# Running the last two units of each layer inside the hardware loop, and keeping the third buffer place for weights, in a two-layer decode kernel

## The chip, the cores and the metric

One core of one Trainium2 chip. The time is the device time of one execution in microseconds (us), the median of several executions. All executions told of here were of the fast state, with a mean granted TensorE clock of 0.669 to 0.675. PE is the matrix engine, ACT and DVE are the scalar and the vector engine, and SP is the engine that issues the loads.

## The reference, cut to what matters

Two layers. Each is attention of one new token over a long cache, followed by a small MLP. There are 2 batches of 32 heads, 64 units of (batch, head) in all, and each unit reads a K and a V of 16384 x 128 bf16, 4 MB each.

```python
def _A_ref(x, k_cache, v_cache, wq, wo):            # B=2, Sq=1, D=576, H=32, Sk=16384, Dh=128
    q = (x @ wq).reshape(B, Sq, H, Dh).transpose(0, 2, 1, 3)
    scores = jnp.einsum("bhqd,bhkd->bhqk", q, k_cache) * (Dh ** -0.5)
    o = jnp.einsum("bhqk,bhkd->bhqd", _softmax(scores), v_cache)
    return o.transpose(0, 2, 1, 3).reshape(B, Sq, H * Dh) @ wo
x = x + _A_ref(_layernorm(x), A_k_cache, A_v_cache, A_wq, A_wo)
x = x + _B_ref(_layernorm(x), B_w1, B_w2, B_w3, B_w4)     # with S = 1, w2 meets only zeros
# ... and both lines once more: the second layer reads the same caches and weights
```

The caches are read twice, except for two units that the second layer finds still in the buffer. That makes 1098 MB of loads with almost no arithmetic per byte.

## The kernel before: what the change and the argument touch

The buffer has three places, each with room for one K and one V. A load is issued by SP, in one fixed order, as soon as the last reader of the bytes under it is done (`Arena.pump`). All loads go to one queue of the DMA.

```python
def place(self, l, i):                    # l: layer, i: position of the unit in the layer
    if i == self.U - 1:
        return 2 - 2 * l                  # the last unit takes the third place
    if l == 0:
        return i % 2
    return (2, 0, 1)[i % 3] if i < self.ROT else (2, 1)[i % 2]      # ROT = 7
# ... (cut) in plan(), the order of the loads:
    for i in range(U):
        kv("K", l, i, ...)
        if l == 1 and i < self.EARLY:     # EARLY = 9: V of a unit right behind its K ...
            kv("V", l, i)
        elif i >= 1 and (l, i - 1) != (1, self.EARLY - 1):
            kv("V", l, i - 1)             # ... later K one unit ahead of V
        if i % 8 == 0 and 8 <= i <= 8 * self.n_wo:
            want_wo(l, i // 8 - 1, wp * self.place_n)    # a piece of wo for 4 heads
    # ... (cut)
    kv("V", l, U - 1, (2, 1, 1))
    want_w34(l, 1, 1 if l == 0 else 2)    # w3, then w4 in four pieces; pieces 2 to 4 lie over w3
```

K of a unit is cut into 16 groups of 8 blocks of 128 rows. PE and ACT do 9 or 10 of these groups (transpose the 8 blocks, evict, multiply with q), while DVE does the rest of the 16 as dot products. Then come the maximum, the exponentials, and 128 small "weighing" matmuls with V. Two units are one turn of a hardware loop on PE, ACT and DVE; units 0 to 1 of layer 1, units 0 to 7 of layer 2, and units 62 and 63 of both are straight-line code.

```python
def attention(self, l):
    first = (2, self.EARLY - 1)[l]
    self.s.loops.append((l * U + first, (U - 2 - first) // 2, 2, ...))
    for i in range(U):
        # ... (cut) turns; weigh(l, i - 1) inside unit i, but not inside the last unit:
        now = i >= 1 and not early and i < U - 1
        # ... (cut)
        if i % 8 == 1 and 9 <= i <= 8 * self.n_wo + 1:
            self.project_piece(l, i // 8 - 1)      # multiplies with a piece of wo
        if i == U - 2:
            self.project_mid(l)
    self.unit_max(l, U - 1)
    self.exps(l, U - 1)
    # ... (cut)
    self.weigh(l, U - 2, 0)
    self.weigh(l, U - 2, 1)
    self.weigh(l, U - 1, 0)
    self.weigh(l, U - 1, 1)
    # ... (cut) then the last head of wo, then the MLP
```

## Time and profile before

| | before |
|---|---|
| time, median of the 3 runs known at the prediction | 2566.87 us |
| span of the profiled run | 2565.0 us |
| data moved by the data queue | 1097.76 MB, 99.8% of the 16 engines' span |
| instruction blocks fetched | 48 of 16 KB |
| rate in undisturbed slices | 431 to 433 GB/s |

The page, kernel before. The first line gives busy us, share and count for each engine; GB/s is the mean over all DMA engines in 40 slices of 64 us; the queue lines give packets, MB and share of 16 engines' time.

```profile
PE 1652.4 (64%) x36879; PEld 1539.2 (60%) x36879; DVE 1750.1 (68%) x2587; ACT 1229.8 (48%) x1941; POOL 0.8 (0%) x10
...
GB/s 414 429 429 431 432 433 430 431 432 432 430 432 431 432 432 432 432 431 431 424 413 429 423 418 432 431 433 431 432 431 432 431 431 433 431 431 431 433 431 375
...
q1 hardware_dynamic: 46712, 1097.76, 99.8%
q8 instruction: 48, 0.79, 0.1%
```

No compute engine is over 68% busy, and the data queue is full. The weak slices are the first, the ones around the change of layers (20 to 24) and the last. Next the timeline of PE at the end of layer 1 (start, length, line, instruction, count; in brackets the idle time ahead of it and what ended it):

```profile
1271.94 5.61 PE L799 MATMUL ops<-p,buf 128*128 128x1 bf16 x205
1279.56 1.52 PE L799 MATMUL ops<-p,buf 128*128 128x1 bf16 x51 [2.02 <-issue]
1281.34 0.29 PE L632 MATMUL misc<-otn,wolast 128*128 128x2 bf16 x5 [0.26 <-DVE otn L821]
1282.09 0.61 PE L562 MATMUL misc<-xa,small 128*128 128x16 f32 x2 [0.46 <-DVE xa L557]
```

After the last exponentials, PE weighs V of units 62 and 63 in one run of 256 matmuls, with a gap of 2.02 us in which nothing in the trace was being waited for. Only then can the MLP begin (L562, at 1282.09). What the DMA did meanwhile, in the table of stretches (each engine's busy us and count, then PE clock, DMA share, GB/s):

```profile
1286.00:1290.00 4.00, 2.12 (x65) 2.00 (x64) 0.99 (x7) 0.50 (x2) 0.00 (x0) 0.50 0.92 374
1290.00:1294.00 4.00, 2.83 (x107) 2.74 (x103) 0.51 (x3) 0.49 (x2) 0.00 (x0) 0.50 0.77 243
```

The rate falls to 243 GB/s: the second piece of w4 has to wait until the MLP has read w3. The queue's own timeline shows when the last K, two V and w3 were issued:

```profile
1212.21 0.43 SPq L403 DMA_DIRECT2D buf<-in_A_k_cache_dram  x1
1229.93 0.33 SPq L403 DMA_DIRECT2D buf<-in_A_v_cache_dram  x1
1253.84 1.28 SPq L400 DMA_DIRECT2D buf<-in_A_v_cache_dram  x3
1255.16 2.99 SPq L417 DMA_DIRECT2D buf<-in_B_w_dram  x5
```

K of unit 63 goes out at 1212.21, well ahead; V of unit 63 (three parts) waits until 1253.84. Finally layer 2: the end of PE's multiplication with the first piece of wo after unit 9, and two of the four stretches of 20 us from 1440 to 1520 (the other two show 415 and 413):

```profile
1483.12 0.69 PE L632 MATMUL misc<-orows,buf 128*128 128x2 bf16 x20 [0.39 <-DVE orows L883]
1484.77 1.89 PE L726 MATMUL tps<-ident,buf 128*128 128x128 bf16 x16 [0.95 <-DVE xa L841]
```

```profile
1440.00:1460.00 20.00, 12.41 (x275) 11.82 (x275) 13.49 (x19) 9.65 (x15) 0.00 (x0) 0.67 0.98 413
1460.00:1480.00 20.00, 12.30 (x275) 11.72 (x275) 13.35 (x19) 9.65 (x15) 0.00 (x0) 0.67 0.99 417
```

PE's product with wo (L632) waits for DVE, not for the load. The rate is about 414 GB/s for 80 us, where 432 is normal. I read this as 3 us lost.

### The profile page before, as it was taken

The page shows a single profiled execution, that of the slowest core. Times are in us where ns is not written, and L with a number is a line of the kernel's source. Part 1 is how long each engine was busy: PE and PEld are TensorE (multiplying, and loading weights), DVE is VectorE, ACT ScalarE, POOL GpSimd, SP SyncE. Part 2 cuts the span into 40 slices and gives each one's busy share as a digit, 9 for nine tenths or more (in the row PEclk, how much of TensorE's full clock was granted, in tenths as well). Part 3 has the DMA queues.
Part 4 walks back from the last instruction along what each step waited for, and adds up shares of the span by engine and source line. Part 5 has one row for each costly group of instructions (what it writes and reads, how often), then busy time and mean ns, then how long its engine had stood idle before and what let it go on. Part 6 is the DMA issues. An engine that isn't in the chain of part 4 may idle for free.

```text
span 2565.0 us, 84163 instructions
## 1 busy us (share of the span) xinstructions
PE 1652.4 (64%) x36879; PEld 1539.2 (60%) x36879; DVE 1750.1 (68%) x2587; ACT 1229.8 (48%) x1941; POOL 0.8 (0%) x10
## 2 busy tenths in 40 slices
PE   5656666666566666656668676666656665666566
PEld 5555665566565656655668665555655655565565
DVE  5666767677666767766658677766766766677664
ACT  4444544454455445544436555444544544454452
POOL 0000000000000000000000000000000000000000
PEclk8666666676667666766656667666666766676665
DMA  9999999999999999999999999999999999999998
GB/s 414 429 429 431 432 433 430 431 432 432 430 432 431 432 432 432 432 431 431 424 413 429 423 418 432 431 433 431 432 431 432 431 431 433 431 431 431 433 431 375
DMA packets 46770, 1098.63 MB, mean 428 GB/s; under 512 B 4916, under 2 KB 6008, under 8 KB 11512
## 3 DMA queue, kind: packets, MB, share of 16 engines
q1 hardware_dynamic: 46712, 1097.76, 99.8%
q8 instruction: 48, 0.79, 0.1%
q14 instruction: 10, 0.08, 0.0%
HBM read 1097.74 MB, written 0.00 MB: 428 GB/s over the span
## 4 chain that ended last, share of the span: by engine, by line
DMA 57%; issue 16%; DVE 16%; PE 8%; SPq 1%; ACT 1%; DVEq 0%
DMA buf<-in_A_k_cache_dram 56%; DVE prod L755 12%; PE tps L726 5%; DVE sd L758 3%; PE misc L774 2%; SPq L434 1%; PE ops L799 1%; DMA buf<-in_B_w_dram 1%; DMA buf<-in_A_wq_dram 1%; SPq L417 0%; ACT ktsb L730 0%; PE misc L632 0%; DVE small L776 0%; PE sps L596 0%; PE sps L743 0%
## 5 line engine op out<-in xcount | busy, mean ns | idle before, releaser
L730 ACT ACTIVATE ktsb<-tps 128x1024 bf16<-128x1024 bf16 x1156 | 1123.3, 1031 | 879.9 <-PE tps L726 875.3
L726 PE MATMUL tps<-ident,buf 128*128 128x128 bf16 x9248 | 908.1, 262 | 619.8 <-DMA buf<-in_A_k_cache_dram 606.9
L726 PEld LDWEIGHTS tps<-ident,buf 128*128 128x128 bf16 x9248 | 732.1, 120 | 648.4 <-DMA buf<-in_A_k_cache_dram 626.4
L758 DVE TENSOR_REDUCE sd<-prod 128x8 f32<-128x1024 bf16 x892 | 1088.0, 1220 | 30.9
L755 DVE TENSOR_TENSOR prod<-buf,qb 128x1024 bf16<-128x1024 bf16 x892 | 607.5, 681 | 11.1 <-DMA buf<-in_A_k_cache_dram 10.2
L799 PE MATMUL ops<-p,buf 128*128 128x1 bf16 x16384 | 461.9, 164 | 65.8 <-DMA buf<-in_A_v_cache_dram 56.4
L799 PEld LDWEIGHTS ops<-p,buf 128*128 128x128 bf16 x16384 | 444.6, 100 | 75.0 <-DMA buf<-in_A_v_cache_dram 64.8
L776 DVE TENSOR_REDUCE small<-misc 128x1 f32<-128x128 f32 x128 | 37.3, 291 | 646.2 <-PE misc L774 646.2
L743 PE MATMUL sps<-qcur,ktsb 128*128 128x1 bf16 x9248 | 397.4, 166 | 113.3 <-ACT ktsb L730 89.4
L743 PEld LDWEIGHTS sps<-qcur,ktsb 128*128 128x128 bf16 x9248 | 348.4, 101 | 177.4 <-ACT ktsb L730 172.0
L710 ACT ACTIVATE qb<-misc 128x128 bf16<-128x128 f32 x128 | 35.5, 277 | 360.7 <-PE misc L707 360.7
L774 PE MATMUL misc<-identS,small 128*128 128x128 f32 x256 | 95.3, 476 | 12.2 <-DVE small L768 12.2
L774 PEld LDWEIGHTS misc<-identS,small 128*128 128x128 f32 x256 | 69.9, 334 | 13.8 <-DVE small L768 13.8
L785 ACT ACTIVATE p<-sps,small 128x72 bf16<-128x72 f32 (+1 forms) x128 | 41.6, 325 | 7.8 <-DVE small L776 7.8
L785 ACT ACTIVATE p<-sd,small 128x56 bf16<-128x56 f32 (+1 forms) x128 | 44.6, 349 | 0.0
L702 ACT ACTIVATE qcur<-qt 128x1 bf16 (+1 forms) x128 | 29.2, 228 | 19.6 <-DVE qt L639 19.6
L868 PE MATMUL misc<-lpiece,small 128*128 128x16 f32 x28 | 8.5, 385 | 42.7 <-DVE lpiece L866 42.7
L707 PE MATMUL misc<-ident,qcur 128*128 128x128 bf16 x128 | 34.2, 267 | 1.1 <-ACT qcur L702 1.1
L868 PEld LDWEIGHTS misc<-lpiece,small 128*128 128x128 f32 x28 | 7.0, 311 | 45.3 <-DVE lpiece L866 45.3
L764 DVE TENSOR_REDUCE small<-sps 128x1 f32<-128x72 f32 (+1 forms) x128 | 28.4, 222 | 0.4 <-PE sps L743 0.4
L785 ACT ACTIVATION_READ_ACCUMULATOR p<-sps,small (+1 forms) x128 | 27.3, 213 | 0.0
L785 ACT ACTIVATION_READ_ACCUMULATOR p<-sd,small (+1 forms) x128 | 26.6, 208 | 0.0
(86 smaller groups left out, 223.5 us busy)
## 6 DMA issues: line engine op xcount, KB each, us to landing
buf<-in_A_k_cache_dram SPq DMA_DIRECT2D x124, 4096.0 KB, 24.3
buf<-in_A_v_cache_dram SPq DMA_DIRECT2D x124, 4096.0 KB, 33.6
buf<-in_B_w_dram SPq DMA_DIRECT2D x8, 1152.0 KB, 26.9
buf<-in_A_wq_dram SPq DMA_DIRECT2D x8, 1024.0 KB, 10.5
buf<-in_A_wo_dram SPq DMA_DIRECT2D x14, 576.0 KB, 34.6
buf<-in_A_k_cache_dram SPq DMA_DIRECT2D x3, 2048.0 KB, 16.5
buf<-in_B_w_dram SPq DMA_DIRECT2D x2, 2160.0 KB, 34.9
buf<-in_A_v_cache_dram SPq DMA_DIRECT2D x2, 2048.0 KB, 27.8
```

Source lines behind the costliest of these rows:

```text
L702: self.act(lambda a, u: a.activation(out=self.qcur[:, q:q + 1], in_=self.qt[:, bass.ds(u, 1)], func=ACT.Copy), r=["qt"], w=[f"qcur{q}"], u=u)
L707: self.pe(lambda pe: pe.matmul(self.misc[:, 0:128], lhsT=bcast(self.qcur[:, q:q + 1], 128), rhs=self.ident[:, :], start=True, stop=True), ...
L710: self.act(lambda a: a.activation(out=self.qb[q][:, :], in_=self.misc[:, 0:128], func=ACT.Copy), r=["P:misc"], w=[f"qb{q}"])
L726: ins = pe.transpose(self.tps[b][:, j * 128:(j + 1) * 128], kt[:, (j0 + j) * 128:(j0 + j + 1) * 128], self.ident[:, :])
L730: self.act(lambda a: a.activation(out=self.ktsb[k][:, :, :].rearrange("p a b -> p (a b)"), in_=self.tps[b][:, :], func=ACT.Copy), r=[f"P:t ...
L743: ins = pe.matmul(self.sps[sp][:, col:col + 1], lhsT=self.ktsb[k][:, j, :], rhs=self.qcur[:, sp:sp + 1], start=True, stop=True)
L755: self.dve(lambda v: v.tensor_tensor(out=self.prod[d][:, :, :], in0=k3, in1=bcast_mid(self.qb[q][:, :], self.CH), op=ALU.mult), r=[*res, f ...
L758: self.dve(lambda v: v.tensor_reduce(out=self.sd[q][:, o:o + self.CH], in_=self.prod[d][:, :, :], axis=AX.X, op=ALU.add), r=[f"prod{d}"], ...
L774: self.pe(lambda pe: pe.matmul(self.misc[:, 128:256], lhsT=bcast(self.m[:, q:q + 1], 128), rhs=self.identS[:, :], start=True, stop=True), ...
L776: self.dve(lambda v: v.tensor_reduce(out=self.bias[:, q:q + 1], in_=self.misc[:, 128:256], axis=AX.X, op=ALU.max, negate=True), r=["P:misc ...
L785: self.act(lambda a, u, c0=c0, c1=c1, src=src: a.activation(out=self.p[q][:, c0:c1], in_=src, func=ACT.Exp, bias=self.bias[:, q:q + 1], sc ...
L799: ins = pe.matmul(self.ops[q][:, 0:1], lhsT=vt[:, j * 128:(j + 1) * 128], rhs=self.p[q][:, h * self.TB + j:h * self.TB + j + 1], start=(h ...
```

## The change

Its intent: units 62 and 63 become a last turn of the loops, so that the code is shorter and unit 62 is weighed inside unit 63. K and V then stay in their two places, and w3 and w4 get the third place to themselves (number 2 in layer 1, number 0 in layer 2). In layer 2, K runs ahead of V from unit 7 rather than 9, and K of unit 7 gets the third place. Its first piece of wo must therefore be loaded later. In the diffs unchanged lines are left out.

```diff
-    EARLY = 9
-    ROT = 7
+    EARLY = 7
+    ROT = 8
-    def place(self, l, i):
-        if i == self.U - 1:
-            return 2 - 2 * l
+    def place(self, kind, l, i):
         if l == 0:
             return i % 2
-        return (2, 0, 1)[i % 3] if i < self.ROT else (2, 1)[i % 2]
+        if kind == "K":
+            return (1, 0, 2)[i % 3] if i < self.ROT else (2, 1)[i % 2]
+        return (1, 0, 2)[i % 3] if i < self.ROT - 1 else (1, 2)[i % 2]
 ... (cut)
-                if i % 8 == 0 and 8 <= i <= 8 * self.n_wo:
-                    want_wo(l, i // 8 - 1, wp * self.place_n)
+                t, r = divmod(i - (10 if (l, i) == (1, 10) else 8), 8)
+                if r == 0 and 0 <= t < self.n_wo and (l, i) != (1, 8):
+                    want_wo(l, t, wp * self.place_n)
-                if l == 0 and i == 6:
+                if l == 0 and i == 1:
                     want_w2(wp * self.place_n + unit)
-            want_w34(l, 1, 1 if l == 0 else 2)
+            want_w34(l, wp, 2)
 ... (cut)
-        return self.NCH // 2 + (1 if i < self.U - 2 else 2)
+        return self.NCH // 2 + 1
 ... (cut)
-        self.s.loops.append((l * U + first, (U - 2 - first) // 2, 2, ...))
+        self.s.loops.append((l * U + first, (U - first) // 2, 2, ...))
-            now = i >= 1 and not early and i < U - 1
+            now = i >= 1 and not early
 ... (cut)
-        self.weigh(l, U - 2, 0)
-        self.weigh(l, U - 2, 1)
-        self.normalize(other, other + 1, self.o[:, other:other + 1], "o")
+        self.normalize(u0, u1, self.o[:, u0:u1], "o")
         self.weigh(l, U - 1, 0)
+        self.project(h0, h1, [(h0, h1 - h0, w, res, lambda: self.ring.done(key))])
         self.weigh(l, U - 1, 1)
```

The rest of the diff lets all turns of a loop raise the same semaphores (the counters by which engines and loads wait for each other), clears two tiles that an idle last iteration now reads, and drops the function for the middle piece of wo.

## The prediction

> **What bounds it now.** The DMA stream. The page shows 99.8% of 16 engines' span on the one data queue, 1097.8 MB at 428 GB/s; the slices of undisturbed stretches stand at 431-433. DVE is 68%, PE 64%, ACT 48% busy. The Trainium skill ("DMA: Bandwidth & Descriptors", Specifications) gives a fabric ceiling of 435 GB/s; the trace's 432 agrees. In the steady loop a K takes 24.3 us from issue to landing and PE waits 5.6 us per unit for it (chain, timeline), so work saved on PE, DVE or ACT there is worth nothing. An estimate: 1097.8 MB at 432 is 2541 us, so only 24 us of the 2565 are not pure streaming. By the window table they lie at: the start (130 GB/s in the first 4 us, 2.8 us lost); the change of layers (1286-1294 us: 374 and 243 GB/s, 2.3 us lost; w3/w4 rows themselves run at about 415); units 8-11 of layer 2 (1440-1520 us: mean 414, about 3 us lost); the end (about 6 us after the last weight lands).
>
> **What the change does.** Bytes are the same; w2 (0.7 MB) only comes earlier.
> 1. Units 62 and 63 of each layer go into the loops: four unrolled units fewer, an estimated 9 fewer 16 KB instruction blocks of the 48 in the queue table: 0.3 us of DMA.
> 2. Third place only for weights. K of unit 63 is issued a unit later (about 1231 instead of 1212 us), but the queue is first-in first-out and full, so it still lands near 1255. V of unit 63 goes at about 1250 instead of 1254. Neither is a loss or gain.
> 3. Tail of attention. Before: m at 1269.5, then 256 weighing matmuls (1271.9 to 1281.1, with a 2.0 us gap the profile calls issue). After: one more DVE chunk in unit 63 (7 dots, not 6: +1.9 us), but unit 62 is already weighed: 128+15 matmuls, about 4 us. MLP should start 1-3 us earlier, so w4's second piece, which waits for w3's first matmuls, is issued earlier and the hole at 1286-1294 shrinks: gain 1-2 us. The Trainium skill ("Runtime: NRT & Kernel Launch", Instruction fetch mechanics) says a taken branch outside the fetched window forces a fetch; the exit of the loop is now right before this tail instead of hidden under a 5.6 us K wait[...]. The trace shows no exposed loop exit either way.
> 4. Layer 2, unit 7: K7 (place 0) and K8 ahead of V7. K8 lands one transfer (9.7 us) earlier, near 1433. But the first piece of wo is now queued after K10 and V9 while it is still multiplied after unit 9; I expect PE to stand some 15 us there (until about 1483), and K12 is issued near 1499 as before. Net gain about 1 us, instead of the 3 that lie there.
> 5. w2 at unit 1: up to 0.3 us in the first 60 us. Extra semaphore counts, query and memsets: nothing.
>
> The end of the run stays bound by w4's landing.
>
> **Predicted: 2564.2 us, 2560.5 to 2567.6 (8 in 10).** Faster by over 2%: 0.01; within 2%: 0.98; slower: 0.01.
>
> **Signs.** Right: data bytes equal; DMA share 99.8% or more; 243 GB/s near 1290 filled to over 330; instruction packets near 39; PE wait for wo after unit 9 of layer 2, with a thin spot near 1502; no 2 us issue gap in the last weighing. Wrong on 3: a gap with nothing waited for at the loop's exit and the same hole. Wrong on 4: no wo wait, or 1440-1520 at 431.
>
> **What would make it wrong.** Loop exits costing many us on PE, ACT and DVE in turn; the wo stall starving the queue for more than 3 us; issue running into a full queue.

## The result, and the profile after

The changed kernel took 2564.06 us (median of 6, 2563.77 to 2564.28); the kernel before, in 6 runs, 2565.86 (2565.40 to 2567.28). The ratio is 0.9992, 95% interval 0.9979 to 1.0005. Ratios are taken like this: a ratio is the mean time of one kernel's fast runs over that of the other's of the same rounds, so it is not quite the ratio of the medians. The two sets of runs don't overlap, and 1.8 us separate their medians. The traced runs stand further apart, 2565.0 and 2562.0 us, because the traced run of before was one of its slower ones (2566.82).

The page after:

```profile
PE 1648.9 (64%) x36813; PEld 1543.0 (60%) x36813; DVE 1756.3 (69%) x2589; ACT 1231.2 (48%) x1941; POOL 1.0 (0%) x12
...
GB/s 410 429 431 432 433 429 432 431 430 433 430 433 432 431 431 432 431 432 432 425 425 428 428 410 430 433 432 429 433 431 431 432 430 433 430 431 433 431 430 387
...
q1 hardware_dynamic: 46712, 1097.76, 99.9%
q8 instruction: 39, 0.64, 0.1%
```

The same 1097.76 MB, and 39 instruction blocks instead of 48. The end of layer 1 on PE:

```profile
1274.19 1.84 PE L812 MATMUL ops<-p,buf 128*128 128x1 bf16 x64
1275.90 0.54 PE L644 MATMUL misc<-otn,buf 128*128 128x2 bf16 x15
1276.30 1.84 PE L812 MATMUL ops<-p,buf 128*128 128x1 bf16 x64
1278.40 0.29 PE L644 MATMUL misc<-otn,wolast 128*128 128x2 bf16 x5 [0.26 <-DVE otn L834]
1279.15 0.61 PE L574 MATMUL misc<-xa,small 128*128 128x16 f32 x2 [0.46 <-DVE xa L569]
```

128 + 15 matmuls, no gap, and the MLP (L574) begins at 1279.15 instead of 1282.09. Leaving the loop just before cost nothing that can be seen: PE's idle times there, 2.52 us up to DVE's maximum and 1.15 us up to ACT's exponentials, were 2.31 and 1.15 us in the kernel before. The stretches and the queue:

```profile
1286.00:1290.00 4.00, 3.51 (x127) 3.42 (x126) 0.35 (x2) 0.23 (x1) 0.00 (x0) 0.50 1.01 400
1290.00:1294.00 4.00, 1.01 (x38) 1.04 (x39) 1.07 (x4) 0.26 (x1) 0.00 (x0) 0.50 1.02 418
```

```profile
1231.23 0.33 SPq L412 DMA_DIRECT2D buf<-in_A_k_cache_dram  x1
1231.90 0.33 SPq L412 DMA_DIRECT2D buf<-in_A_v_cache_dram  x1
1247.69 2.94 SPq L409 DMA_DIRECT2D buf<-in_A_v_cache_dram  x3
1250.67 7.85 SPq L426 DMA_DIRECT2D buf<-in_B_w_dram  x5
```

The hole of 243 GB/s is gone. K of unit 63 was issued 19 us later and unit 63 still began at 1255.51, against 1255.17 before. In layer 2:

```profile
1471.20 0.33 PE L882 MATMUL misc<-opiece,ident 128*32 128x2 bf16 x16 [0.99 <-DVE opiece L876]
1482.86 0.69 PE L644 MATMUL misc<-orows,buf 128*128 128x2 bf16 x20 [11.33 <-DMA buf<-in_A_wo_dram]
1484.55 1.89 PE L739 MATMUL tps<-ident,buf 128*128 128x128 bf16 x16 [1.00 <-DVE xa L854]
```

```profile
1492.00:1496.00 4.00, 3.60 (x124) 3.43 (x125) 3.93 (x5) 3.09 (x5) 0.00 (x0) 0.89 0.72 311
1496.00:1500.00 4.00, 3.15 (x67) 2.88 (x64) 3.93 (x5) 1.95 (x3) 0.00 (x0) 0.50 0.46 197
```

PE now stands 11.33 us for the first piece of wo. K and V of units 12 and 11 are issued only at 1499.09 and 1499.46, and the rate falls to 197 GB/s: a hole as deep as the one that was closed. By mean rates it costs (432-311) x 4/432 + (432-197) x 4/432 = 3.3 us. Yet unit 13 of layer 2 starts at 1531.41, 1.93 us ahead of before (1533.34), where it was 1.62 us ahead at unit 6 (1402.18 against 1403.80). So either the hole stole a larger gain, or it cost nothing. The experiments were made to find out.

### The profile page after: what moved, and what is told of

It reads as the page before. It is cut to its first block, busy times and chain, and to the rows that moved or that the text cites. A ratio compares the mean times of both kernels' runs of the same rounds, so it can differ in the third digit from the quotient of the medians.

```text
span 2562.0 us, 84308 instructions
## 1 busy us (share of the span) xinstructions
PE 1648.9 (64%) x36813; PEld 1543.0 (60%) x36813; DVE 1756.3 (69%) x2589; ACT 1231.2 (48%) x1941; POOL 1.0 (0%) x12
## 3 DMA queue, kind: packets, MB, share of 16 engines
q1 hardware_dynamic: 46712, 1097.76, 99.9%
## 4 chain that ended last, share of the span: by engine, by line
DMA 60%; issue 16%; DVE 14%; PE 8%; SPq 1%; ACT 1%; ACTq 0%; DVEq 0%
DMA buf<-in_A_k_cache_dram 55%; DVE prod L768 12%; PE tps L739 5%; DVE sd L771 2%; DMA buf<-in_B_w_dram 2%; PE misc L787 1%; DMA buf<-in_A_v_cache_dram 1%; DMA buf<-in_A_wo_dram 1%; PE ops L812 1%; DMA buf<-in_A_wq_dram 1%; SPq L426 0%; ACT ktsb L743 0%; SPq L443 0%; PE sps L756 0%; PE misc L644 0%
## 5 line engine op out<-in xcount | busy, mean ns | idle before, releaser
L768 DVE TENSOR_TENSOR prod<-buf,qb 128x1024 bf16<-128x1024 bf16 x896 | 610.4, 681 | 11.2 <-DMA buf<-in_A_k_cache_dram 10.3
L798 ACT ACTIVATE p<-sps,small 128x72 bf16<-128x72 f32 x128 | 41.4, 323 | 6.7 <-DVE small L789 6.7
L798 ACT ACTIVATE p<-sd,small 128x56 bf16<-128x56 f32 x128 | 44.4, 347 | 0.0
L777 DVE TENSOR_REDUCE small<-sps 128x1 f32<-128x72 f32 x128 | 28.4, 222 | 0.4 <-PE sps L756 0.2
```

The source lines that it names most:

```text
L768: self.dve(lambda v: v.tensor_tensor(out=self.prod[d][:, :, :], in0=k3, in1=bcast_mid(self.qb[q][:, :], self.CH), op=ALU.mult), r=[*res, f ...
L798: self.act(lambda a, u, c0=c0, c1=c1, src=src: a.activation(out=self.p[q][:, c0:c1], in_=src, func=ACT.Exp, bias=self.bias[:, q:q + 1], sc ...
```

## The experiments

Eight kernels were run, all correct. Where "over the changed kernel" is said, medians of different rounds are compared; the kernel before was run in all rounds and its medians were 2565.86, 2566.14, 2565.86 and 2566.05, so such a difference is good to some 0.3 us.

### e1: take the wait for wo away

In layer 2 all pieces of wo are loaded at units 10, 18, ... and multiplied after units 11, 19, ... .

```diff
-                t, r = divmod(i - (10 if (l, i) == (1, 10) else 8), 8)
-                if r == 0 and 0 <= t < self.n_wo and (l, i) != (1, 8):
+                t, r = divmod(i - (8, 10)[l], 8)
+                if r == 0 and 0 <= t < self.n_wo:
-            if i % 8 == 1 and 9 <= i <= 8 * self.n_wo + 1:
-                self.project_piece(l, i // 8 - 1)
+            t, r = divmod(i - (9, 11)[l], 8)
+            if r == 0 and 0 <= t < self.n_wo:
+                self.project_piece(l, t)
 ... (cut: the same shift in the call that sets up the loop)
```

> The changed kernel, with the pieces of wo in layer 2 multiplied two units later (after units 11, 19, ... instead of 9, 17, ...) and loaded after units 10, 18, ... . Theory (the 11.3 us that PE stands for the first piece of wo after unit 9 of layer 2 delay K12 until the DMA queue is empty at 1493-1500 us, which costs about 3 us): the wait is gone, K12 is issued near 1486 instead of 1499, no slice of 4 us between 1480 and 1510 under 380 GB/s, and the time is 2.5 to 3 us below the changed kernel, 2561 to 2562 us. Rival (the empty queue comes of the order K ahead of V and of having only two places, so it returns wherever the transfers run out): a slice under 330 GB/s remains between 1480 and 1520 and the time stays within 1 us of the changed kernel.

Measured: 2563.41 us (2563.34 to 2563.54), ratio to before 0.9989 (0.9976 to 1.0003). The wait and the hole are both gone: PE goes from unit 9 to unit 10 with an ordinary wait for K, and the two stretches show 410 and 442. Timeline of PE at the start of unit 10, then stretches:

```profile
1471.58 1.67 PE L739 MATMUL tps<-ident,buf 128*128 128x128 bf16 x14 [5.20 <-DMA buf<-in_A_k_cache_dram]
```

```profile
1492.00:1496.00 4.00, 3.56 (x38) 3.50 (x39) 1.07 (x3) 2.19 (x3) 0.00 (x0) 0.52 0.95 410
1496.00:1500.00 4.00, 3.34 (x72) 2.82 (x69) 3.93 (x5) 4.00 (x9) 0.00 (x0) 1.00 1.03 442
```

But the time is only 0.65 us below the changed kernel, and unit 13 starts at 1531.30, against 1531.41. My theory falls: a hole of 3.3 us by mean rates was removed and at most 0.1 us came of it there. Of the rival, the time came true (within 1 us), but its cause falls too, as the hole did not return.

What a mean rate hides are the 16 DMA engines. The trace holds 16 updates of its semaphore for each load (4880 for the 305 loads compared in the kernel before). I read each as the landing of one engine's share. (Which engine is which is not recorded; the times are sorted, so that the last landings belong to the same engine is a reading too.) For three loads in a row around the hole:

```
                              first     median    last  (landing of the 16 shares, us)
changed kernel   K of unit 11 1484.55   1489.07   1492.54
                 V of unit 10 1494.25   1498.76   1502.22
                 K of unit 12 1510.82   1510.92   1511.94
e1               K of unit 11 1484.43   1488.95   1492.39
                 V of unit 10 1494.14   1498.67   1502.11
                 K of unit 12 1503.86   1508.38   1511.82
```

In the changed kernel the engines are 8 us apart. The first runs dry at 1494 and the last is busy until 1502.22. K12 was issued at 1499.09, in time for the slowest, which lands it 9.72 us after its share of V10, exactly a load's length. The hole is the faster engines waiting for the slowest, and every consumer waits for the slowest in any case. In e1 they stay apart and the slowest lands K12 at 1511.82. **The measure of a loss is the time between the slowest engine's landings, over 9.71 us per 4 MB.** By that measure the two traced kernels differ as follows, in all gaps between landings of a whole K or V that exceed 9.71 us by more than 0.15:

```
before   1.35 at 26, 1.58 at 95, 1.13 at 1404, 1.12 at 1475, seven smaller ones: 7.5 us in all
changed  1.46 at 26, 1.49 at 97, 1.55 at 1402, 1.56 at 1462, one of 0.38:        6.4 us in all
```

Next to these stands the change of layers. The slowest engine's landings of w4's first and second piece lie 6.18 us apart before (1292.47 to 1298.65) and 4.22 after (1292.86 to 1297.08): 2.0 us. The sum, 1.1 + 2.0, is the 3.0 us between the two spans. The losses of about 1.5 us were unexplained so far. They coincide with packets of the instruction queue: 16 KB each, all the 48 of before lying at the start, around the change of layers, in the first units of layer 2 and at the end, wherever new code is entered. An obvious rival, that a load was issued late, is excluded by the traces: at every such gap of more than 1 us, in these two kernels and in all eight experiments, the late load had been issued at least 4.6 us before the slowest share of the load ahead of it landed.

The 2.0 us at the change of layers are not all the hole's either. In the kernel before, 15 shares of w4's second piece had landed by 1297.53, and only the last came at 1298.65, after an instruction block fetched at 1290.47. So about 1.1 of the 2.0 us look like a block's cost.

### e2: put the tail back

Units 62 and 63 are unrolled again, V of unit 62 is weighed after unit 63, as before; places and loads as changed.

```diff
+        return self.NCH // 2 + (1 if i < self.U - 2 else 2)
+        self.s.loops.append((l * U + first, (U - 2 - first) // 2, 2, ...))
+            now = i >= 1 and not early and i < U - 1
+            if i == U - 2:
+                self.project_mid(l)
+        self.weigh(l, U - 2, 0)
+        self.weigh(l, U - 2, 1)
         self.weigh(l, U - 1, 0)
 ... (cut: `project_mid` comes back, and what stood in its place goes)
```

> The changed kernel with units 62 and 63 of each layer unrolled behind the loop again, and V of unit 62 weighed after unit 63, as before; places and order of loads stay as changed. Theory (the hole at the change of layers was closed because the MLP starts 3 us earlier, as only 128 and not 256 weighing matmuls stand between the last exponentials and it): the MLP starts about 3 us later, a slice of 4 us near 1290 us falls under 300 GB/s again, and the time is 2 to 3 us above the changed kernel, 2566 to 2567. Rival (the hole was closed because V of unit 63 and w3 are issued 6 us earlier, with the third place free): no such slice, and the time stays within 1 us of the changed kernel.

Measured: 2566.21 us (2564.99 to 2567.62), ratio to before 1.0002 (0.9988 to 1.0015): 2.15 us over the changed kernel, as the theory said. The MLP begins at 1281.92, 2.8 us later than in the changed kernel, though V of unit 63 is issued as early as there (1247.91), and the hole is back:

```profile
1286.00:1290.00 4.00, 2.11 (x67) 2.00 (x67) 0.99 (x7) 0.50 (x2) 0.00 (x0) 0.50 0.92 377
1290.00:1294.00 4.00, 2.84 (x103) 2.75 (x100) 0.49 (x3) 0.49 (x2) 0.00 (x0) 0.50 0.81 278
```

So the earlier start of the MLP fills this hole, and the earlier issue of V63 and w3 does not. But the time again is not that of the hole: in this traced run the slowest engine's landings of w4's pieces lie 4.27 us apart (1292.91 to 1297.18), hardly more than the 4.22 without a hole. (The traced run, 2564.99 us, is the fastest of the five, so it may not speak for the slower ones.) And this kernel has 48 instruction blocks again. e2 alone can't say how much is the tail's order and how much the code.

### e3 and e4: the order of K and V

e3 is the changed kernel with `EARLY = 9`; e4 has that and e1's change.

> The changed kernel with one constant as before: K runs ahead of V from unit 9 of layer 2, not from unit 7. Theory (while PE stands for the first piece of wo, landing in the same place of the same queue, the order of K and V ahead of it gains nothing): PE still waits for wo after unit 9, K12 is issued near 1498, and the time is within 0.7 us of the changed kernel. Rival (the order is what gained): 1 us or more slower than the changed kernel.

> e1 and e3 together: wo two units later, K ahead from unit 9 only. Theory: without the wait for wo, the order begins to matter: K11 is issued only about 5 us before the queue runs dry (near 1476), so slices of 340 to 390 GB/s near 1480, and a time 0.5 to 1.5 us above e1 but below the changed kernel. Rival (the order never matters): equal to e1 within 0.4 us.

Measured: e3 2564.15 us (2564.01 to 2564.36), ratio 0.9992 (0.9978 to 1.0006); e4 2563.34 us (2563.11 to 2563.85), ratio 0.9989 (0.9975 to 1.0003). e3 equals the changed kernel, as expected, although PE waits only 2.31 us for wo there instead of 11.33. e4 equals e1, which its rival said: stretches of 328 and 340 GB/s do appear in e4 near 1455, and cost nothing. Letting K run ahead two units earlier is worth nothing either way.

### e5 and e6: instruction blocks, nothing else

The loop of layer 1 begins at unit 30, or 16, instead of 2. Work and order stay; more of it is straight-line code.

```diff
-        first = (2, self.ROT)[l]
+        first = (30, self.ROT)[l]          # e6: 16
```

> The changed kernel with the loop of layer 1 beginning at unit 30 instead of 2: the same work in the same order, but 28 more units of straight-line code. From 48 to 39 blocks for four units, that is an estimated 63 more instruction blocks of 16 KB, 102 in all. Theory (a block of instructions goes to one of the 16 DMA engines and holds up that engine's share of the data by about 1.5 us, as the landing times of the slowest engine show; the slowest engine sets the time): about 4 blocks on each engine, so unit 62 of layer 1 starts about 6 us later and the time is 4.5 to 7.5 us above the changed kernel, 2568.5 to 2571.5. Rival (blocks cost their bytes, 1.03 MB at 432 GB/s): 2.4 us or less, at most 2566.5. Second rival (PE stalls on issue cost the time): PE waits for K under 2 us per unit in the unrolled stretch, and time well above 2572.

> As e5 with the loop of layer 1 beginning at unit 16: an estimated 32 more blocks, about 2 on each engine. Theory: 2 to 4 us above the changed kernel, 2566 to 2568, about half of what e5 loses. Rival (bytes): 1.2 us, at most 2565.3.

Measured: e5 2575.22 us (2574.98 to 2575.52), ratio 1.0035 (1.0018 to 1.0051), with 100 blocks; e6 2569.92 us (2569.83 to 2570.20), ratio 1.0015 (0.9998 to 1.0031), with 70. That is 11.2 us for 61 more blocks and 5.9 us for 31: 0.18 and 0.19 us per block. Both times lie above the ranges of the theory: it has the mechanism and the proportion, and its size is too small by nearly half. Both rivals fail. The bytes of 61 blocks are 1.0 MB, 2.3 us at 432 GB/s. The delay arises in the unrolled stretch: unit 62 of layer 1 starts at 1246.83 in e5, 10.6 us later than in the changed kernel (1236.23). And the time is not PE's. It had ten gaps at the weighing matmuls in which it waited for nothing in the trace (16.1 us in all), but its slack took them up: its waits for K in the unrolled stretch are as long as in the loop (us in total, times, longest; 100 to 620 us, first e5, then the changed kernel):

```profile
PE tps L739 <- DMA buf<-in_A_k_cache_dram: 129.1, 26, 7.1
PE ops L812 <- issue: 16.1, 10, 2.6
```

```profile
PE tps L739 <- DMA buf<-in_A_k_cache_dram: 134.3, 23, 7.2
```

The instruction queue of e5, and PE's timeline where one unit takes 21.05 us (377.14 to 398.19) instead of the usual 19.4:

```profile
q8 instruction: 100, 1.64, 0.3%
```

```profile
377.14 1.86 PE L739 MATMUL tps<-ident,buf 128*128 128x128 bf16 x16 [0.48 <-DMA buf<-in_A_k_cache_dram]
...
398.19 1.89 PE L739 MATMUL tps<-ident,buf 128*128 128x128 bf16 x16 [5.33 <-DMA buf<-in_A_k_cache_dram]
```

PE waits 5.33 us for a K that came late. The landing times show why the cost is twice my estimate. In e5, after these blocks, the 16 shares of a load land (relative to the first) at 0, 0.0, 0.2, 0.3, 0.5, 0.5, 2.7, 5.1, 12.1, 12.3, 12.3, 12.4, 12.4, 12.4, 12.5 and 12.8 us (607 us), where the changed kernel's last is at 3.3. So eight shares are far behind and the others hardly. I had assumed 16 engines in turn; by these times about eight take the blocks in turn, each of them losing about 1.5 us. This is inferred, as the trace names no engine. By estimate, one step of 1.5 us for every eight blocks is 0.19 us per block. A count agrees: between 100 and 640 us the slowest engine's landings show no gap of more than 1 us over 9.71 in the changed kernel, three in e6 (31 blocks more), and seven in e5 (61 more).

### e7: the block count of before, with the changed tail

The loop of layer 1 begins at unit 6 (`first = (6, self.ROT)[l]`), which brings 48 blocks.

> The changed kernel with the loop of layer 1 beginning at unit 6: four more unrolled units, so about the 48 instruction blocks of the kernel before, with the changed end of each layer kept. e5 and e6 measured 11.2 us for 61 blocks and 5.9 us for 31, 0.18 to 0.19 us per block. Theory (two separate gains: fewer blocks, and the hole at the change of layers closed): 1.5 to 1.9 us above the changed kernel, so 2565.6 to 2566.0, with no hole near 1290 us. Rival A (e2's 2.1 us is the hole alone and blocks in this number fall on other engines than the slowest): within 0.5 us of the changed kernel. Rival B (e2's 2.1 us is blocks alone): as e2, 2566.2, hole or no hole. This run can't tell theory and B apart by time alone if it lands near 2566; the landing times of the slowest engine around 1290 us must.

Measured: 2565.48 us (2565.37 to 2565.59), ratio to before 0.9998 (0.9984 to 1.0011): 1.42 us over the changed kernel, 0.16 us per block, just under the range of the theory. Between 100 and 640 us its landings show one gap of more than 1 us (at 177), where the changed kernel has none. Rival A is out. There is no hole:

```profile
1286.00:1290.00 4.00, 3.80 (x135) 3.78 (x136) 0.39 (x3) 0.00 (x0) 0.00 (x0) 0.50 0.98 384
1290.00:1294.00 4.00, 0.89 (x34) 0.80 (x31) 1.26 (x4) 0.49 (x2) 0.00 (x0) 0.50 0.98 388
```

Rival B is not settled. The test named beforehand, the slowest engine's landings, does not part it from the theory: w4's first two pieces land 4.18 us apart here (1294.35 to 1298.53), and 4.27 in e2. By medians e2 lies 0.7 us above e7, but from different rounds, and e2's own runs scatter from 2564.99 to 2567.62. The fairer pair is before and e7, of the same rounds and with 48 blocks each: 2566.05 against 2565.48, and eight of the nine runs of before (2565.71 and above) lie above all five of e7 (2565.59 and below). So of the change's 1.8 us about 1.4 go with the number of blocks. The remaining 0.4 to 0.6 go with the rest of the change together; that it is the order of the tail, and not where the blocks fall, is not shown.

### e8: fewer blocks still

The third place rotates only up to unit 5 of layer 2, so the loop begins at unit 6 and two units fewer are unrolled. Place 0 is then free for the first piece of wo at unit 8.

```diff
-    ROT = 8
+    ROT = 6
-        if kind == "K":
-            return (1, 0, 2)[i % 3] if i < self.ROT else (2, 1)[i % 2]
-        return (1, 0, 2)[i % 3] if i < self.ROT - 1 else (1, 2)[i % 2]
+        return (1, 0, 2)[i % 3] if i < self.ROT else (1, 2)[i % 2]
-                t, r = divmod(i - (10 if (l, i) == (1, 10) else 8), 8)
-                if r == 0 and 0 <= t < self.n_wo and (l, i) != (1, 8):
+                t, r = divmod(i - 8, 8)
+                if r == 0 and 0 <= t < self.n_wo:
-            want_w34(l, wp, 2)
+            want_w34(l, wp, 2 - l)
```

> A try at beating both: the third place rotates for K and V only up to unit 5 of layer 2, so its loop can begin at unit 6 and two units fewer are unrolled; the first piece of wo is loaded at unit 8 again, as place 0 is free by then. By 0.19 us per block and an estimated 4 to 5 blocks fewer (34 to 35): 0.8 us below the changed kernel, 2563.2. Against it: K7 must wait for unit 5, as in the kernel before, where the slowest engine stood about 1.1 us at 1464-1475 us; if that returns, 2564.3 or more.

Measured: 2563.11 us (2563.02 to 2563.30), ratio to before 0.9989 (0.9975 to 1.0002). It is the fastest of all, 0.95 us below the changed kernel:

```profile
q8 instruction: 35, 0.57, 0.1%
```

There are four blocks fewer than in the changed kernel, and the loss of 1.56 us at 1462 is absent from the slowest engine's landings, as is the gap of 1.1 us near 1475 that was feared. But e8 is no test of blocks alone: with wo at unit 8 again, PE's wait of 11.33 us for it is gone too, and e1, which only removed that wait, gained 0.65 us with all its 39 blocks.

All kernels by their blocks. At equal blocks the medians still differ by up to 0.8 us, so a few blocks can't be read from the time alone:

| kernel | blocks | median us |
|---|---|---|
| e8 | 35 | 2563.11 |
| e4 | 39 | 2563.34 |
| e1 | 39 | 2563.41 |
| changed | 39 | 2564.06 |
| e3 | 39 | 2564.15 |
| e7 | 48 | 2565.48 |
| before (six runs) | 48 | 2565.86 |
| e2 | 48 | 2566.21 |
| e6 | 70 | 2569.92 |
| e5 | 100 | 2575.22 |

## Why the prediction was right, and where it was not

The time (2564.2 predicted, 2564.06 measured) and the verdict were right, but the closeness of the time was partly luck. The prediction took 2.7 us off 2566.87, the median of the three runs known then; six runs put the kernel before at 2565.86, so the gain was 1.8 us, and a base 1.0 us too high hid that 2.7 was too much. And in the sum behind it two terms were wrong in opposite directions.

- **Bound.** Right: the data queue stays at 99.9%, with the same bytes. But the "24 us that are not pure streaming" were placed by mean rates, and the 3 us at 1440-1520 us were not a loss of that size: in e1 and e4 it changed nothing whether such thin stretches were there, and by the slowest engine's landings the kernel before lost 1.3 us in them (1.12 and 0.20). The end, put at about 6 us after the last weight lands, is 3.9 us (2561.14 to 2565.04).
- **Step 1, the instruction blocks.** The saving was named (nine blocks fewer, exactly 39), but its size was off by about five: 0.3 us predicted, from bytes spread over 16 engines, the reading that failed as a rival in e5. e5 and e6 measured 0.18 to 0.19 us per block, e7 1.42 us for as many as these nine. This is the mis-sized term, and the largest part of the gain.
- **Step 2, K63 and V63.** Right: issue at 1231 and 1248 (predicted 1231 and 1250), unit 63 begins at 1255.51.
- **Step 3, the tail.** Right in its course: the MLP starts 2.9 us earlier, the 2 us gap is gone, the loop's exit costs nothing, 243 GB/s became 418. Its gain was put at 1 to 2 us. In the traced pair the slowest engine gained 2.0, of which about 1.1 look like an instruction block's; by medians at equal blocks 0.6 (before less e7) or 0.7 (e2 less e7) are left for it and whatever else differs there. The hole of e2's traced run cost its slowest engine next to nothing (4.27 against 4.22). How often the hole of before costs something was not settled; the wider scatter of before and e2 may be this, but that is only argued.
- **Step 4, unit 7 of layer 2.** The course was right to the microsecond (PE waits until 1482.86, predicted 1483; K12 at 1499.09, predicted 1499). The step that failed is "Net gain about 1 us, instead of the 3 that lie there". The order itself gains nothing clear (0.1 us, e3). And my first explanation of the result, that the wo wait ate 3 us, failed in e1: only 0.65 us came of removing it, none of it by unit 13. e1's gain arises at the end: there the changed kernel's engines are level (1.2 us apart) and a block delays the slowest by 0.55 us (landings at 2535.21 and 2538.54, 3.33 apart; e1: 2.79), whereas in e1 they are 8.2 us apart and the blocks fall on engines with time to spare. That rests on one pair of traces; e4's traced run (2563.85) was no faster than that of the changed kernel (2563.87) and can't confirm it.
- **Step 5.** Nothing, as said: unit 10 of layer 1 starts at 196.00 us, against 195.75 before; e1 with the same code there has 195.76.

The Trainium skill ("Runtime: NRT & Kernel Launch", Instruction fetch mechanics) says that instructions come in 16 KiB blocks over the sequencer's own DMA queue and that crossing into a new block is mostly hidden. The trace agrees on the blocks (35 to 100 packets of 16384 bytes). On the cost the runs differ: PE could afford it (PE's waits for K in e5 are those of the loop), and the data queue paid for it, 0.18 us a block. The same section prefers full unrolling because of branches; in this kernel the loop wins, as 14 more turns of straight-line code cost 11.2 us and no exposed loop exit is in the trace. The skill ("DMA: Bandwidth & Descriptors", Queues, rings and completion order) says each DMA engine serves its queue rows in turn, a packet at a time; the delay of a single share by about 1.5 us when a block passes fits that, though no trace here names the engine that carried a block. "Perfetto Trace Analysis" (Identifying the Most-Contended Engine) warns that 16 DMA engines make occupancy misleading; here the mean rate misled in the same way.

## What to carry to other kernels

In a kernel bound by loads, judge a hole in the mean DMA rate by the landing of the slowest engine, as faster engines that ran dry cost nothing here while the slowest had work. Straight-line code was not free here even where no compute engine lost time by it: as the runs read, its blocks ride on the same DMA engines and delay the share that everything waits for. So roll code up in load-bound stretches, and when a change "saves nothing", count the instruction blocks.

## What the Trainium skill lacked or had wrong

- "Runtime: NRT & Kernel Launch", Instruction fetch mechanics: an instruction block was not hidden here, where the data queue is the limit. By the landing times it held up one DMA engine's share by about 1.5 us, and the time grew by 0.18 us per block (11.2 us for 61 blocks, 5.9 for 31). The page's preference for full unrolling is wrong for this kernel.
- The same section, or "DMA: Bandwidth & Descriptors": no page says on which DMA engines the blocks land. By the landing times of e5, about eight of the 16 took them, and these fell 12 us behind the rest over 28 units.
- "Perfetto Trace Analysis", What "DMA-bound" means: it names specific DMA engines as one possible limit, but lacks that DMA engines drift apart (1 to 13 us here) and that a hole in the mean rate can be drift alone. The hole of 311 and 197 GB/s in the changed kernel cost the slowest engine nothing: 9.72 us between its landings.
